# First chunk's two first half-width blocks written ahead of the third batch's recurrence

## The chip, the cores and the metric

The kernel runs on one core of a Trainium2 chip. The metric is the device time of one execution in microseconds (us). Engines are named as in the profile: PE is TensorE's matmul, PEld its weight load, DVE VectorE, ACT ScalarE, POOL GpSimd, SP SyncE, which issues most of the DMAs here.

## What is computed

An mLSTM recurrence over 4 batches, 8 heads, 768 steps and a head size of 40, and behind it two gated feed-forward layers on its output, all in float32:

```python
C = f_stab * C + i_stab * outer(v, k)     # per batch and head, step by step
n = f_stab * n + i_stab * k
y = sigmoid(o_gate) * (C @ q) / max(abs(n @ q), 1)
x = y as 3072 tokens x 320
x = (sigmoid(x @ w_gate) * (x @ w_val)) @ w_out       # d_ff 1536
h = x @ w_in                                          # d_ff 2048
out = (h * clip(h + 3, 0, 6) / 6) @ w_out2
```

## The kernel before

**Chunks.** The 768 steps are cut into 6 chunks (`NC`) of 128 steps. Inside a chunk the recurrence is done as matrix products, batch by batch; between chunks a state per batch is carried. A chunk gives 512 tokens (`T`): 4 batches of 128, batches 0 and 1 in the first half of the columns, 2 and 3 in the second.

**A batch of the recurrence** has three pieces. `att0`: scores on TensorE (L361), decays as scans on VectorE (L387), values scaled by ScalarE (L350) or VectorE (L352), the scores weighted on VectorE (L402). `att1`: the outputs on TensorE (L454, L469), the denominators (L491 to L495) and the gated product (L352, L503) on VectorE, the state (L521 to L529). `att2`: transposes on TensorE (L535), and the split into a high and a low part, `XH` on ScalarE (L540) and `XL` on VectorE (L541). Matmuls take their operands in such two parts, three products each.

**The first feed-forward layer** goes over 12 blocks (`F1`) of 128 hidden columns for each chunk. `m1_h(c, f, ts)` makes a block's two products from the tokens `ts` (16 matmuls in `h_pair`, L553 to L560, into two banks of PSUM), the sigmoid (L579, ScalarE), the product with the second bank (L580, VectorE), and the split of the result by `split_g` (L566 ScalarE, L567 VectorE). `m1_out` adds a block's 8 matmuls (L595, L605) into three accumulator banks; it is written one block behind `m1_h`. For chunk 0 the first 4 blocks are done in half widths: blocks 0 to 3 of `steps` take the tokens of batches 0 and 1, blocks 4 to 7 those of batches 2 and 3; from step 8 on a block has all 512 columns.

**Weights** arrive as 64-bit words of float64 and are turned into float32 by `scaled` (L100, ScalarE) and `to_f32` (L117, L120, VectorE), then split by `hi_in` (L141, L143, ScalarE) and `lo_in` (L149, L153, VectorE), or by `hi_out1` (L163) and `lo_out1` (L169, L172) for the output weights. `jobs` lists these conversions; `work(n, limit)` writes the next n of them, each with its fetch (L90).

**Order.** A first part, in `tc.manual_schedule()`, is ordered by hand: batches 0 and 1 of chunk 0, the first two input tiles (`w0`, `w1_`) and the first output tile (`wo_`), and last the state of the two batches. Each engine keeps the written order of these instructions. The rest is written in a loop over `steps`; a planner orders it for each engine by its own estimate of when operands are ready, and also puts such instructions between those of the hand-ordered part. In that loop `quota[i]` says how many pieces of the recurrence are written ahead of step i (batches 2 and 3 of chunk 0 first, then the next chunks'), and `work` follows each step.

**Buffers.** PSUM has 3 banks for blocks (`ps_mm`), 3 accumulators (`ps_acc`) and 2 for the recurrence (`ps_att`); the hand-ordered part takes all 8 in turn, and keeps one of `ps_mm` and one of `ps_acc` until `state(0, b)` has read them.

Of the kernel before, what the change touches and what calls it, by code (L numbers as in the profile page):

```python
# [26 lines left out]
T = B * L  # L27
F1 = 1536 // P
# [4 lines left out]
def mlstm_then_two_gated_ffn(  # L33
# [71 lines left out]
    def to_f32(r, u=None):  # L105

        lower = r.bitcast(I32).rearrange("p (n two) -> p two n", two=2)[:, 0, :]
        u = scaled(r) if u is None else u
        bits = gpool.tile([P, 640], I32, tag="bits", name="bits")
        nc.vector.tensor_scalar(  # L117
            out=bits, in0=u.bitcast(I32), scalar1=3, scalar2=None, op0=ALU.logical_shift_left
        )
        nc.vector.scalar_tensor_tensor(  # L120
            out=bits, in0=lower, scalar=29, in1=bits,
            op0=ALU.logical_shift_right, op1=ALU.bitwise_or,
        )
        return bits.bitcast(F32)
# [21 lines left out]
    def lo_in(w, x):  # L146
        wf = w.bitcast(F32)
        xm = x[:, 0:512].rearrange("p (j n) -> p j n", j=2)
        nc.vector.tensor_tensor(  # L149
            out=w[:, :, 384:640], in0=xm, in1=wf[:, :, 0:256], op=ALU.subtract  # L150
        )
        for j, a, b in halves_in:
            nc.vector.tensor_tensor(  # L153
                out=w[b, j, 256:384], in0=x[a, 512:640], in1=wf[a, j, 256:384], op=ALU.subtract
            )
# [4 lines left out]
    def hi_out1(key, x):  # L160

        w = new_slot(key)
        nc.scalar.copy(out=w[:, :, 0:320], in_=x.rearrange("p (j n) -> p j n", j=2))  # L163
        return w

    def lo_out1(w, x):
        wf = w.bitcast(F32)
        r = x.rearrange("p (j n) -> p j n", j=2)
        nc.vector.tensor_tensor(  # L169
            out=w[:, :, 320:384], in0=r[:, :, 256:320], in1=wf[:, :, 256:320], op=ALU.subtract  # L170
        )
        nc.vector.tensor_tensor(  # L172
            out=w[:, :, 384:640], in0=r[:, :, 0:256], in1=wf[:, :, 0:256], op=ALU.subtract
        )
# [399 lines left out]
    def m1_h(c, f, ts):  # L574
        n = ts.stop - ts.start
        banks = [ps_mm()[:, :n], ps_mm()[:, :n]]
        h_pair(slots["in", f], (1, c), banks, ts)
        g = gpool.tile([P, T], F32, tag="g", name="g")[:, :n]
        gate = nc.scalar.activation(out=g, in_=banks[0], func=AF.Sigmoid).ins  # L579
        nc.vector.tensor_tensor(out=g, in0=g, in1=banks[1], op=ALU.mult)  # L580
        gs[c, f, ts.start] = split_g(g)
        return gate

    def m1_out(c, f, ts):
        if f == 0 and ts.start == 0:
            acc1[c] = [ps_acc() for _ in range(3)]
        a = [bank[:, ts] for bank in acc1[c]]
        w = slots["out", f // 2][:, f % 2, :]
        gh, gl = gs.pop((c, f, ts.start))

        st, en = f == 0 and ts.start == 0, f == F1 - 1
        for m in range(2):
            hi, lo = w[:, m * P : (m + 1) * P], w[:, 384 + m * P : 384 + (m + 1) * P]
            for lhsT, rhs in ((hi, gh), (hi, gl), (lo, gh)):
                nc.tensor.matmul(  # L595
                    out=a[m], lhsT=lhsT, rhs=rhs, start=st and lhsT is hi and rhs is gh,
                    stop=en and lhsT is lo, skip_group_check=True,
                )

        tail = [  # L600
            dict(out=a[2], lhsT=w[:, 256:384], rhs=gh, start=st, stop=en),
            dict(out=a[2][0:64], lhsT=w[:, 256:320], rhs=gl, start=False, stop=False),
        ]
        for kw in tail if f == 0 else reversed(tail):
            nc.tensor.matmul(**kw, skip_group_check=True)  # L605

    def m1_end(c):
        a = acc1.pop(c)
        x2 = xpool.tile([P, 3, T], F32, tag="x2", name="x2")
        for m in range(2):  # L610
            nc.scalar.copy(out=x2[:, m, :], in_=a[m])

        sw = gpool.tile([P, T], F32, tag="g", name="sw")
        nc.scalar.copy(out=sw[0:64], in_=a[2][64:128])
        nc.scalar.copy(out=sw[64:128], in_=a[2][0:64])
        nc.vector.tensor_tensor(out=x2[:, 2, :], in0=sw, in1=a[2], op=ALU.add)
        nc.sync.dma_start(out=x2_dram[c], in_=x2)
# [28 lines left out]
    def work(count, limit):  # L646

        for _ in range(count):
            if len(jobs) > n_jobs - limit:
                src, use, key = jobs.pop()  # L650
                r = fetched.pop(0) if fetched else fetch(src)
                use(key, to_f32(r) if src.dtype == I64 else r)
# [9 lines left out]
    with tc.manual_schedule():  # L662
        qk_load(0, 0)
        vko_load(0, 0)
        qk_load(0, 1)
        raws = [fetch(jobs[-1][0])]
        vko_load(0, 1)
        for _ in stabilise(0, L):
            pass
        nc.sync.dma_start(out=fz_dram[0], in_=fz[:, 0, :])  # L670
        raws += [fetch(jobs[-2][0]), fetch(jobs[-3][0])]
        for b in range(2, B):
            qk_load(0, b)
            vko_load(0, b)
            dec_load(0, b)
        later = stabilise(L, S)
        first, second = spread(0), spread(1)
        next(later)
        next(later)
        next(first)  # L680
        transpose_rows(i_c, iT, range(0, 1))
        decays(0, 0, 0)
        next(first)
        next(later)
        next(later)
        decays(0, 0, 1)
        scores(0, 0, any_ps)
        value_ones(0, 0)
        values(0, 0, False)
        u = scaled(raws[0])  # L690
        values_end(0, 0, False)
        next(later)
        next(later)
        for n in range(2):
            weigh(0, 0, n)
            next(second)
        x0 = to_f32(raws[0], u)
        scores(0, 1, any_ps)
        for n in range(2):
            decays(0, 1, n)  # L700
        value_ones(0, 1)
        values(0, 1, False)
        values_end(0, 1, False)
        for b in range(2):
            out_gate(0, b)
        w0 = hi_in(jobs.pop()[2], x0)
        outputs(0, 0, any_ps)
        for n in range(2):
            weigh(0, 1, n)
        outputs(0, 1, any_ps)  # L710
        gated(0, 0, denominators(0, 0), False)
        u = scaled(raws[1])
        lo_in(w0, x0)
        gated(0, 1, denominators(0, 1), False)
        for b in range(2):
            opened = att2(0, b, any_ps)
        x1 = to_f32(raws[1], u)
        w1_ = hi_in(jobs.pop()[2], x1)
        u = scaled(raws[2])
        lo_in(w1_, x1)  # L720
        x2_ = to_f32(raws[2], u)
        wo_ = hi_out1(jobs.pop()[2], x2_)
        lo_out1(wo_, x2_)
        for b in range(2):
            state(0, b)

# [19 lines left out]
        pieces.append((c, B - 1, 2))  # L746
    n_first = len(tile_steps(0))

    quota = [2, 2] + [1] * 4 + [0, 1] * 4 + [1] * (n_first - 14) + [1, 1, 0, 1, 0, 1]
    quota += [1] * (len(steps) - len(quota))  # L750
    before = []
    for i, (c, f, ts) in enumerate(steps):
        if i == halves[0] - 1:
            for b in range(2):
                att_load(1, b)
                dec_load(1, b)
        for _ in range(quota[i]):
            if pieces:
                cp, b, piece = pieces.pop(0)
                if cp > 0 and b == 0 and piece == 0:  # L760
                    x_tiles((1, cp))
                with ExitStack() as queued:
                    for ins in opened if cp == 0 else ():
                        queued.enter_context(tc.issue_after(ins))
                    (att0, att1, att2)[piece](cp, b, ps_att)
                nxt = divmod(cp * B + b + 2, B)
                if cp > 0 and piece == 2 and nxt[0] < NC:
                    att_load(*nxt)
                    dec_load(*nxt)
        gate = m1_h(c, f, ts)  # L770
        if before:
            m1_out(*before)
            if before[1] == F1 - 1:
                m1_end(before[0])
        before = (c, f, ts)
        if c == 0:
            work(1 if i < 2 * halves[0] else 2, n_w1)
        elif c < NC - 1:

            with tc.issue_after(gate):  # L780
                work(c > 1 and f % 2 == 0, n_conv)
        elif f == 0:
            work(F2, n_conv)
        else:
            work(f > 1, n_jobs)
        if c == NC - 1 and f == 6:
            x_split(0)
# [125 lines left out]
```

## Time and profile before

| | us |
|---|---|
| runs shown | 871.9, 872.7, 873.03 (median 872.7) |
| profiled execution, its own time | 872.27 |
| its span in the profile | 870.5 |

The span is what the trace covers, from the first to the last event on the core; the execution's own time has 1.8 us around it. Times of rows are counted from the start of the span.

### The profile page before, as it was taken

How to read it: one execution, taken by the hardware profiler on the slowest of the kernel's cores; microseconds unless marked ns; L12 is line 12 of the kernel's file. 1: busy time of each engine (PE TensorE's matmuls, PEld its weight loads, DVE VectorE, ACT ScalarE, POOL GpSimd, SP SyncE). 2: the span in 40 equal slices, each digit the busy share in tenths (PEclk: the TensorE clock that was granted, in tenths of full speed). 3: DMA queues.
4: the chain of work that ended last, by engine and by line, in shares of the span. 5: the costliest groups of instructions: out<-in, count | busy, mean ns of one | idle time of the engine just before them, and what ended most of it. 6: DMA issues, size and time to landing. Idle time of an engine off the chain costs nothing.

```text
span 870.5 us, 16999 instructions
## 1 busy us (share of the span) xinstructions
PE 845.0 (97%) x7205; PEld 727.3 (84%) x7205; DVE 502.7 (58%) x898; ACT 358.6 (41%) x721; POOL 2.5 (0%) x8
## 2 busy tenths in 40 slices
PE   6599999999999999999999999999999999999998
PEld 6488778887878778878888888999999999999997
DVE  7899966665676666567545544344343353443433
ACT  3688634222333333332226445343343343433333
POOL 1000000000000000000000000000000000000000
PEclk9999999999999999999999999999999999999999
DMA  9636623331444355445103321001010010000000
GB/s 348 236 124 222 218 96 110 104 112 72 154 163 163 132 189 165 170 175 169 68 1 97 91 82 73 1 31 37 1 67 1 1 67 1 31 1 2 31 1 30
DMA packets 24923, 83.43 MB, mean 96 GB/s; under 512 B 2576, under 2 KB 5840, under 8 KB 24848
## 3 DMA queue, kind: packets, MB, share of 16 engines
q1 hardware_dynamic: 24800, 82.26, 27.7%
q8 instruction: 56, 0.92, 0.4%
q14 instruction: 19, 0.16, 0.1%
q10 hardware_dynamic: 48, 0.10, 0.0%
HBM read 68.35 MB, written 13.99 MB: 95 GB/s over the span
## 4 chain that ended last, share of the span: by engine, by line
PE 82%; DVE 10%; DMA 3%; issue 2%; ACT 2%; DVEq 0%; ACTq 0%; SPq 0%
PE mm L557 11%; PE mm L559 11%; PE mm L558 11%; PE acc L595 9%; PE mm L553 6%; PE mm L560 5%; PE acc L819 5%; PE acc L818 5%; PE acc L817 5%; PE acc L605 3%; DMA dec<-fz_dram 2%; PE att L361 2%; DVE dec L387 2%; PE att L819 2%; PE att L817 2%
## 5 line engine op out<-in xcount | busy, mean ns | idle before, releaser
L557 PE MATMUL mm<-xh,w 128*128 128x512 f32 (+1 forms) x520 | 195.7, 376 | 0.1
L558 PE MATMUL mm<-xl,w 128*128 128x512 f32 (+1 forms) x520 | 194.9, 375 | 0.0
L559 PE MATMUL mm<-xh,w 128*128 128x512 f32 (+1 forms) x520 | 194.8, 375 | 0.0
L566 ACT CAST gh<-g 128x512 fp32r<-128x512 f32 (+1 forms) x178 | 106.2, 597 | 214.1 <-DVE g L580 122.6
L567 DVE TENSOR_TENSOR gl<-g,gh 128x512 fp32r<-128x512 f32 (+1 forms) x178 | 117.6, 661 | 113.3 <-ACT gh L566 113.0
L799 DVE SCALAR_TENSOR_TENSOR g<-g,mm 128x512 f32<-128x512 f32 x96 | 66.0, 687 | 112.2 <-ACT g L798 112.2
L558 PEld LDWEIGHTS mm<-xl,w 128*128 128x128 f32 x520 | 98.5, 189 | 18.4
L559 PEld LDWEIGHTS mm<-xh,w 128*128 128x128 f32 x520 | 98.3, 189 | 18.5
L798 ACT ACTIVATE g<-mm,half 128x512 f32<-128x512 f32 x96 | 66.2, 690 | 112.1 <-PE mm L560 112.0
L557 PEld LDWEIGHTS mm<-xh,w 128*128 128x128 f32 x520 | 98.6, 190 | 14.4 <-issue 0.3
L595 PE MATMUL acc<-gh,w 128*128 128x512 f32 (+1 forms) x328 | 104.4, 364 | 2.2 <-ACT gh L566 2.2
L553 PE MATMUL mm<-xl,w 128*128 128x512 f32 (+1 forms) x260 | 104.2, 401 | 0.0
L560 PE MATMUL mm<-xh,w 128*128 128x512 f32 (+1 forms) x260 | 97.2, 374 | 0.0
L819 PE MATMUL acc<-w,gl 128*128 128x320 f32 x288 | 89.0, 309 | 0.0
L818 PE MATMUL acc<-w,gh 128*128 128x320 f32 x288 | 88.9, 309 | 0.0
L817 PE MATMUL acc<-w,gh 128*128 128x320 f32 x288 | 88.8, 308 | 0.0
L580 DVE TENSOR_TENSOR g<-g,mm 128x512 f32<-128x512 f32 (+1 forms) x82 | 50.5, 615 | 56.5 <-PE mm L560 55.9
L579 ACT ACTIVATE g<-mm 128x512 f32<-128x512 f32 (+1 forms) x82 | 44.7, 545 | 69.8 <-PE mm L560 69.4
L595 PEld LDWEIGHTS acc<-gh,w 128*128 128x128 f32 x328 | 60.4, 188 | 12.3 <-ACT gh L566 2.6
L595 PE MATMUL acc<-gl,w 128*128 128x512 f32 (+1 forms) x164 | 60.4, 369 | 1.6 <-DVE gl L567 1.4
L387 DVE TENSOR_TENSOR_SCAN dec<-dec,ident 128x512 f32<-128x512 f32 x40 | 47.7, 1214 | 23.5 <-DMA dec<-fz_dram 23.5
L553 PEld LDWEIGHTS mm<-xl,w 128*128 128x128 f32 x260 | 49.2, 189 | 9.1 <-issue 0.2
(155 smaller groups left out, 1078.2 us busy)
## 6 DMA issues: line engine op xcount, KB each, us to landing
raw<-in_w SPq DMA_DIRECT2D x20, 640.0 KB, 4.2
qk<-in_qkT SPq DMA_DIRECT2D x22, 512.0 KB, 5.1
vko<-in_vko SPq DMA_DIRECT2D x22, 480.0 KB, 4.9
dec<-fz_dram SPq DMA_DIRECT2D x20, 512.0 KB, 6.1
raw<-in_wo SPq DMA_DIRECT2D x14, 640.0 KB, 4.0
w_dram<-bits SPq DMA_DIRECT2D x16, 320.0 KB, 2.4
raw<-w_dram SPq DMA_DIRECT2D x16, 320.0 KB, 3.0
x_dram<-x SPq DMA_DIRECT2D x6, 768.0 KB, 4.5
```

The source lines that it names most:

```text
L553: nc.tensor.matmul(out=banks[j], lhsT=tail, rhs=xl[:, 2, :], start=True, stop=False)
L557: nc.tensor.matmul(out=banks[j], lhsT=hi, rhs=xh[:, k, :], start=False, stop=False)
L558: nc.tensor.matmul(out=banks[j], lhsT=hi, rhs=xl[:, k, :], start=False, stop=False)
L559: nc.tensor.matmul(out=banks[j], lhsT=lo, rhs=xh[:, k, :], start=False, stop=False)
L560: nc.tensor.matmul(out=banks[j], lhsT=tail, rhs=xh[:, 2, :], start=False, stop=True)
L566: nc.scalar.copy(out=gh, in_=g)
L567: nc.vector.tensor_tensor(out=gl, in0=g, in1=gh.bitcast(F32), op=ALU.subtract)
L595: nc.tensor.matmul(out=a[m], lhsT=lhsT, rhs=rhs, start=st and lhsT is hi and rhs is gh, stop=en and lhsT is lo, skip_group_check=True,)
L798: nc.scalar.activation(out=g[j], in_=banks[j], func=AF.Relu, scale=1.0 / 6.0, bias=half)
L817: nc.tensor.matmul(out=a, lhsT=gh[:, ts], rhs=hi, start=st, stop=False)
L818: nc.tensor.matmul(out=a, lhsT=gh[:, ts], rhs=lo, start=False, stop=False)
L819: nc.tensor.matmul(out=a, lhsT=gl[:, ts], rhs=hi, start=False, stop=en)
```

## The change

The half-width blocks 0 and 1 (`m1_h`) and the output product of block 0 (`m1_out`) are written inside the hand-ordered part: block 0 behind the low part of the second input tile, block 1 behind the high part of the first output tile, the output product behind that tile's low part. The loop over `steps` begins at step 2, with `before` set to step 1. The two conversions that `work` wrote behind steps 0 and 1 are written together ahead of the loop, and the six pieces of the recurrence that were written ahead of steps 0 to 3 (2, 2, 1, 1) are written ahead of steps 2 and 3 (3, 3).

```diff
--- before.py
+++ after.py
@@ -718,9 +718,13 @@
         w1_ = hi_in(jobs.pop()[2], x1)
         u = scaled(raws[2])
         lo_in(w1_, x1)
+
+        m1_h(0, 0, slice(0, T // 2))
         x2_ = to_f32(raws[2], u)
         wo_ = hi_out1(jobs.pop()[2], x2_)
+        m1_h(0, 1, slice(0, T // 2))
         lo_out1(wo_, x2_)
+        m1_out(0, 0, slice(0, T // 2))
         for b in range(2):
             state(0, b)
 
@@ -746,10 +750,11 @@
         pieces.append((c, B - 1, 2))
     n_first = len(tile_steps(0))
 
-    quota = [2, 2] + [1] * 4 + [0, 1] * 4 + [1] * (n_first - 14) + [1, 1, 0, 1, 0, 1]
+    quota = [0, 0, 3, 3] + [1] * 2 + [0, 1] * 4 + [1] * (n_first - 14) + [1, 1, 0, 1, 0, 1]
     quota += [1] * (len(steps) - len(quota))
-    before = []
-    for i, (c, f, ts) in enumerate(steps):
+    before = steps[1]
+    work(2, n_w1)
+    for i, (c, f, ts) in list(enumerate(steps))[2:]:
         if i == halves[0] - 1:
             for b in range(2):
                 att_load(1, b)
@@ -768,10 +773,9 @@
                     att_load(*nxt)
                     dec_load(*nxt)
         gate = m1_h(c, f, ts)
-        if before:
-            m1_out(*before)
-            if before[1] == F1 - 1:
-                m1_end(before[0])
+        m1_out(*before)
+        if before[1] == F1 - 1:
+            m1_end(before[0])
         before = (c, f, ts)
         if c == 0:
             work(1 if i < 2 * halves[0] else 2, n_w1)
```

## Rows read from the trace of the kernel before

**Rows 1.** The page, busy time, share of the span and instructions of each engine.

```profile
PE 845.0 (97%) x7205; PEld 727.3 (84%) x7205; DVE 502.7 (58%) x898; ACT 358.6 (41%) x721; POOL 2.5 (0%) x8
```

**Rows 2.** Windows: stretch, length, busy us (instructions) by engine, granted clock, DMA.

```profile
27.50:40.80 13.30, 5.93 (x119) 5.13 (x119) 13.21 (x27) 9.30 (x28) 0.00 (x0) 1.00 0.54 164
40.80:58.90 18.10, 17.76 (x230) 16.14 (x222) 17.27 (x40) 17.44 (x58) 0.00 (x0) 1.00 0.48 163
58.90:77.80 18.90, 16.74 (x242) 15.72 (x241) 18.25 (x42) 12.28 (x36) 0.00 (x0) 0.91 0.62 216
77.80:105.20 27.40, 27.26 (x247) 22.18 (x245) 26.50 (x55) 19.55 (x46) 0.00 (x0) 1.00 0.61 204
105.20:130.00 24.80, 24.80 (x258) 19.92 (x259) 16.55 (x33) 10.71 (x31) 0.00 (x0) 1.00 0.35 113
```

**Rows 3.** Timeline of PE from 25 us: start, length, what, idle before.

```profile
27.38 2.67 PE L361 MATMUL att<-early 40*128 40x128 f32 x16 [0.38 <-ACT iT L284]
35.65 0.36 PE L454 MATMUL att<-vi,early 128*32 128x41 f32 x8 [5.60 <-DVE early L402]
...
40.83 0.58 PE L553 MATMUL mm<-xl,w 128*128 128x256 f32 x1
...
41.42 0.41 PE L558 MATMUL mm<-xl,w 128*128 128x256 f32 x1
41.63 0.41 PE L559 MATMUL mm<-xh,w 128*128 128x256 f32 x1
...
43.28 0.28 PE L560 MATMUL mm<-xh,w 128*128 128x256 f32 x1
43.40 0.28 PE L553 MATMUL mm<-xl,w 128*128 128x256 f32 x1
...
58.97 0.39 PE L553 MATMUL mm<-xl,w 128*128 128x256 f32 x1
```

**Rows 4.** Groups of DVE instructions, 27.5 to 78 us: busy us, mean ns.

```profile
L120 DVE SCALAR_TENSOR_TENSOR bits<-raw,bits 128x640 int32<-128x640 int32 x10 | 8.1, 809 | 0.0
...
L117 DVE TENSOR_SCALAR bits<-u 128x640 int32<-128x640 int32 x10 | 4.8, 480 | 0.1
L149 DVE TENSOR_TENSOR w<-bits,w 128x512 fp32r<-128x512 f32 x6 | 4.0, 672 | 0.0
L153 DVE TENSOR_TENSOR w<-bits,w 64x128 fp32r<-64x128 f32 x12 | 3.4, 286 | 0.3
L580 DVE TENSOR_TENSOR g<-g,mm 128x256 f32<-128x256 f32 x8 | 3.3, 407 | 0.6 <-PE mm L560 0.6
L567 DVE TENSOR_TENSOR gl<-g,gh 128x256 fp32r<-128x256 f32 x7 | 2.9, 417 | 0.4 <-ACT gh L566 0.4
```

**Rows 5.** Timeline of DVE, third batch's second weighting and fourth batch's end.

```profile
38.38 0.67 DVE L402 TENSOR_TENSOR early<-att,early 128x512 f32<-128x512 f32 x1
...
57.27 0.56 DVE L541 TENSOR_TENSOR xl<-att,xh 128x384 fp32r<-128x384 f32 x1
```

**Rows 6.** Timeline of PE, 68 to 75 us.

```profile
68.42 0.28 PE L560 MATMUL mm<-xh,w 128*128 128x256 f32 x1
70.27 0.50 PE L595 MATMUL acc<-gh,w 128*128 128x256 f32 x2 [1.57 <-ACT gh L566]
71.36 0.39 PE L595 MATMUL acc<-gl,w 128*128 128x256 f32 x1 [0.58 <-DVE gl L567]
...
74.41 0.41 PE L558 MATMUL mm<-xl,w 128*128 128x256 f32 x1
74.62 0.41 PE L559 MATMUL mm<-xh,w 128*128 128x256 f32 x1
```

**Rows 7.** Timeline of ACT, 66 to 70 us.

```profile
66.27 0.68 ACT L529 COPY cst<-cst 40x164 f32<-40x164 f32 x2 [1.61 <-DVE cst L524]
66.97 0.39 ACT L579 ACTIVATE g<-mm 128x256 f32<-128x256 f32 x1
...
69.83 0.39 ACT L566 CAST gh<-g 128x256 fp32r<-128x256 f32 x1
```

## The prediction

> **What bounds the kernel now.** I read the page first: TensorE is busy 845.0 us of the span of 870.5 [rows 1]. So a gain can only come out of the places where TensorE is not packed. Next I cut the span into stretches by what runs in them (the windows view), and then read the timelines of the engines inside the stretches that are not packed.
>
> The stretches say this [rows 2]. From 77.8 us on TensorE is packed: 27.26 of 27.40 us, then 24.80 of 24.80. Behind that nothing touched by the change matters, as long as the blocks arrive no later. From 27.5 to 40.8 us TensorE is busy 5.93 of 13.30 and ScalarE 9.30, but VectorE is full: 13.21 of 13.30. From 40.8 to 58.9 all three are full: TensorE 17.76, VectorE 17.27, ScalarE 17.44 of 18.10. From 58.9 to 77.8 TensorE has holes again (16.74 of 18.90) and VectorE does not (18.25). And from 105.2 to 130 VectorE is down to 16.55 of 24.80: by then the weight conversions are done.
>
> The reader is to see that the end time is the moment at which TensorE's packed run begins, plus a constant. That moment depends on two gates. The first is the last instruction of the fourth batch's recurrence, L541 on VectorE, which ends at 57.27 + 0.56 = 57.83 [rows 5]. The second half of the tokens (blocks 4 to 7 of the list of steps) can't start without it, and block 4 does start at 58.97 [rows 3]. The second gate is the path from block 4 to about 77.8, with TensorE's waits of 1.57 and 0.58 us at 70.27 and 71.36 [rows 6].
>
> TensorE's idle stretch is plain in its timeline [rows 3]: scores of the third batch at 27.38, then nothing until 35.65, 5.60 us of it a wait for L402 on VectorE (the weighting of the third batch's scores). The first block starts at 40.83. Its matmuls follow each other by 0.21 us at first (41.42, 41.63) and by 0.12 later (43.28, 43.40): 256 columns at 1.2 and at 2.4 GHz.
>
> **The change part by part.**
>
> *Blocks 0 and 1 and the first output product.* They need the tokens of batches 0 and 1 and the first three weight tiles, which the hand-ordered section makes anyway. On TensorE they are 16 + 16 + 8 = 40 matmuls; at 0.12 us that is 4.8 us, which leaves the stretch from 40.8 on. It goes into 27.5 to 40.8, where 13.30 - 5.93 = 7.4 us are free. At 0.21 us each, as the first ones run now after the idle time, they take 8.4 us, 1.0 more than is free. I cost this at nothing because VectorE's queue covers it; if that cover were gone it would be 1.0 us.
>
> *What a block carries on ScalarE and VectorE.* On ScalarE one sigmoid and one cast, 0.39 us each [rows 7], so 2 x 0.78 = 1.56 us for two blocks. They go from a stretch in which ScalarE is full to one with 4.0 us free: hidden. On VectorE one product (0.407) and one subtraction (0.417) [rows 4], 2 x 0.82 = 1.65 us. They go from a full stretch into a full stretch. VectorE does no less work than before up to the fourth batch's L541, only in another order. Its idle time in both stretches is 0.09 + 0.83 = 0.92 us [rows 2], and that is all that a new order of the same work can win on VectorE itself. The lower bound is nothing. I take 0.5 us, the middle.
>
> *What is queued behind them.* In the hand-ordered section each engine keeps the written order. So the conversion of the third weight tile and the reading of the state (both written behind block 0 or 1) now wait for the block's chain: matmuls, sigmoid, product, cast, subtraction. Without overlap this adds 0.407 + 0.39 + 0.417 = 1.2 us a block, 2.4 us for two; with the third batch's scans filling the waits, only VectorE's own 1.65. The third batch's second L402, which now ends at 38.38 + 0.67 = 39.05 [rows 5], moves back by 1.7 to 2.4 us. The output product also has to wait until the state of batch 1 has been read out of its accumulator bank (three banks, one of them still held); that wait is new for a product written this early, but it lies in TensorE's idle time.
>
> *The two weight tiles written ahead.* `work(2)` now stands ahead of the third batch's three pieces. A tile costs VectorE 0.480 + 0.809 + 0.672 + 2 x 0.286 = 2.53 us [rows 4], two cost 5.1. If the planner takes them first, L402 moves back by up to 5.1 us more; if it uses them as filler, as it does today, by nothing. They are finished before the fourth batch's L541 in either order, so again the sum on VectorE is the same.
>
> *The fetches.* The queue of loads keeps its order: third and fourth weight tile, then the second output tile, then chunk 1's loads. The second output tile's fetch waits for the raw buffer of the tile whose conversion moved back by 1 to 2 us. I cost that at nothing: that tile's columns are wanted far later, at the third block's output product.
>
> *From the third batch's weighting to the fourth batch's L541* it is now 57.83 - 39.05 = 18.8 us. Blocks 0 and 1 lie between its links today; without them it has 1.65 us less on VectorE, 1.56 less on ScalarE, 4.8 less on TensorE. It starts 1.7 to 2.4 us later and is at least 1.65 shorter: 0 to 0.8 us of loss if only VectorE's share comes out, a gain if ScalarE's or TensorE's share was in series with it. I take the two as cancelling.
>
> The sum: 0 (TensorE, ScalarE) - 0.5 (VectorE's idle time) + 0 (start against length) = -0.5 us. The profiled execution took 872.27 us (span 870.5 and 1.8 around it), so 871.8; the median of the runs shown is 0.4 above that execution, so **872.2 us**. A measurement of this kernel tells about 0.2%, 1.7 us, from no change, so this counts as the same.
>
> A rule speaks against the change. TensorE is taken out of the full stretch and will have holes there, and after holes its matmuls run slowly: after the waits at 70.27 and 71.36 they follow by 0.21 us (74.41, 74.62), with a granted clock of 0.91 over that stretch [rows 2, 6]. The Trainium skill (TensorE: Matmul & The Clock Gate, What's actually happening) has it that the throttled state is the default and activity is what lifts it; the trace agrees with its 0.21 after idle time and 0.12 in packed stretches. What it would cost is the third rival below.
>
> **The rivals.**
>
> *Faster: the recurrence was held up by the blocks.* In 40.8 to 58.9 ScalarE and TensorE are as full as VectorE. If the recurrence of the two batches was slowed by queueing behind blocks 0 and 1 there, fourth-batch L541 and block 4 come earlier by 1.65 us (VectorE's share) up to 4.8 (TensorE's). A new order can also dissolve the hold-up at 68.42 to 71.36, worth 1.57 + 0.58 us of waits and about ten matmuls at 0.21 instead of 0.12 (0.9): 3.0 us. VectorE could then put off conversions, since it has 8.2 us free after 105.2. For it: three full engines. Against it: VectorE is full from 27.5 on, and it starts later. The gain is 2 to 4.8 us, 867.9 to 870.7, in the middle 869.3.
>
> *Slower: the third batch falls behind.* The blocks' chain and two tiles of weights ahead of it put L402 back by 1.7 to 2.4 + 5.1 = 7.5 us, and the fourth batch follows the third. Half of it is given back as the same work no longer lies in between. ScalarE's and VectorE's queues work in order, as the sigmoid at 66.97 shows: it stood behind L529, which had waited 1.61 us [rows 7]. It decides once L541 of the fourth batch ends more than 1.7 us after 57.83. Price 2 to 4 us: 874.7 to 876.7.
>
> *Slower: the clock.* Block 4 and the scores ahead of it start at half the clock after holes. Block 4's 16 matmuls cost 16 x 0.09 = 1.4 us more, and the scores (16 matmuls) as much at most: 1.4 to 2.8 us, 874.1 to 875.5.
>
> *The change does nothing:* the planner could leave all as it was around the recurrence, and blocks 0 and 1 just wait earlier. Time 872.7.
>
> **How the numbers follow.** Cancelling, as summed: 0.37. Nothing at all: 0.03. Faster: 0.36. Third batch behind: 0.17. Clock: 0.07. So faster by over 0.2% has 0.36, within 0.2% 0.40, slower 0.24. The range goes from 868.3 (the faster rival's outer end, less its last tenth) to 876.0 (most of the slower one). The likeliest case alone is 870.9 to 874.4.
>
> **What the profile after would show.** Right: blocks' matmuls at about 28 to 38 us, TensorE over 10 us busy in 27.5 to 40.8; VectorE full on both sides; the fourth batch's L541 within a microsecond and a half of 57.8, block 4 right behind it, and the first full-width block within that of 77.8. The faster rival: that L541 at 55 or earlier, or no wait at 70. The slower ones: L541 past 59.5, or 0.21 between block 4's matmuls. What would make me wrong most easily is the planner: it gives the rest of the work another order, and the stretch from 59 to 78 us hangs on which instruction stands ahead of which.

## The result, and the profile after

The changed kernel takes 881.82 us (median of 4 runs, 880.27 to 884.91) against 872.3 of the kernel before (4 runs): a ratio of 1.0116, 95% interval 1.0097 to 1.0134. I had forecast 872.2 and a range up to 876.0. It is slower, and by more than any rival said. The profiled execution is one of 880.27 us with a span of 878.5, so 8.0 us above the span before.

The stretches of the changed kernel (windows; columns as in [rows 2]):

```profile
27.50:40.80 13.30, 10.58 (x80) 9.38 (x83) 13.01 (x28) 9.62 (x30) 0.00 (x0) 0.98 0.47 165
40.80:58.90 18.10, 15.30 (x173) 12.00 (x165) 13.52 (x29) 12.43 (x40) 0.00 (x0) 0.69 0.56 183
58.90:77.80 18.90, 17.87 (x289) 16.02 (x289) 16.14 (x38) 11.30 (x33) 0.00 (x0) 0.86 0.32 110
77.80:105.20 27.40, 26.50 (x267) 22.02 (x266) 26.74 (x54) 21.37 (x54) 0.00 (x0) 1.00 0.61 197
105.20:130.00 24.80, 23.87 (x185) 18.61 (x187) 16.74 (x35) 11.99 (x34) 0.00 (x0) 1.00 0.34 122
```

Against [rows 2]: from 27.5 to 40.8 us TensorE now has 10.58 us of work instead of 5.93, as the change says. But from 40.8 to 58.9 VectorE is down from 17.27 to 13.52 and ScalarE from 17.44 to 12.43, and the granted clock is 0.69 instead of 1.00. All three engines had been full there; now all three wait for each other. VectorE's timeline in that time (start, length, what, idle before):

```profile
43.46 0.69 DVE L149 TENSOR_TENSOR w<-bits,w 128x512 fp32r<-128x512 f32 x1 [0.64 <-ACT w L141]
44.19 0.60 DVE L153 TENSOR_TENSOR w<-bits,w 64x128 fp32r<-64x128 f32 x2
44.82 0.82 DVE L120 SCALAR_TENSOR_TENSOR bits<-raw,bits 128x640 int32<-128x640 int32 x1
45.56 0.68 DVE L402 TENSOR_TENSOR early<-att,early 128x512 f32<-128x512 f32 x1
...
53.51 0.56 DVE L541 TENSOR_TENSOR xl<-att,xh 128x384 fp32r<-128x384 f32 x1 [0.34 <-ACT xh L540]
...
60.77 0.69 DVE L402 TENSOR_TENSOR early<-att,early 128x512 f32<-128x512 f32 x1 [4.70 <-PE att L361]
...
68.50 0.55 DVE L541 TENSOR_TENSOR xl<-att,xh 128x384 fp32r<-128x384 f32 x1
```

The third batch's second L402 ends at 46.24 instead of 39.05 [rows 5], 7.2 us later: between its first L402 (42.15) and this one VectorE now works on two further weight tiles (L149, L153, L120). The third batch's L541 follows at 53.51. Then VectorE stands idle for 4.70 us ahead of the fourth batch's second L402, for scores from TensorE, and the fourth batch's L541 ends at 69.05 instead of 57.83: 11.2 us later. TensorE in that time:

```profile
29.14 0.58 PE L553 MATMUL mm<-xl,w 128*128 128x256 f32 x1
...
37.97 0.39 PE L595 MATMUL acc<-gh,w 128*128 128x256 f32 x1 [1.59 <-ACT w L163]
...
44.62 0.36 PE L553 MATMUL mm<-xl,w 128*128 128x256 f32 x1 [0.22 <-DVE w L153]
...
50.20 0.39 PE L595 MATMUL acc<-gh,w 128*128 128x256 f32 x1 [2.58 <-ACT w L163]
...
50.57 0.41 PE L595 MATMUL acc<-gh,w 128*128 128x256 f32 x1
50.78 0.41 PE L595 MATMUL acc<-gl,w 128*128 128x256 f32 x1
...
57.00 0.35 PE L469 MATMUL mm<-vd,early 128*32 128x41 f32 x4
57.28 0.58 PE L559 MATMUL mm<-xh,w 128*128 128x256 f32 x1
57.79 0.35 PE L469 MATMUL mm<-vd,early 128*32 128x41 f32 x4
...
58.58 2.07 PE L361 MATMUL att<-early 40*128 40x128 f32 x8
...
70.19 0.38 PE L553 MATMUL mm<-xl,w 128*128 128x256 f32 x1
```

Block 0 starts 11.7 us earlier than in [rows 3] (29.14), block 1 9.2 us (34.20 instead of 43.40). Block 2 starts at 44.62, and its output product waits 2.58 us at 50.20 for L163, the conversion of the second output tile on ScalarE:

```profile
49.44 0.71 ACT L163 CAST w<-bits 128x640 fp32r<-128x640 f32 x1
```

Behind that wait matmuls follow by 0.21 us (50.57, 50.78). The fourth batch's second eight scores (58.58) stand behind block 3 and L469, the third batch's state, which alternate: four L469 and one of the block's matmuls take 0.79 us together (57.00, 57.79). The scores themselves need 2.07 us. Block 4 starts at 70.19 instead of 58.97, and the first full-width block (block 8) at 85.92 instead of 77.82: of 11.2 us, 3.1 are won back; the hold-up of [rows 6] is shorter this time (a wait of 0.87 us at 80.25 instead of 1.57 and 0.58, and no matmuls at 0.21 behind it). From block 8 to the end it takes as long as before: +8.1 at block 8, +8.0 at the end.

TensorE takes its matmuls in the order of its queue: the PSUM bank that these scores go to was free at 54.07, when the third batch's L541 had read it, and yet they started at 58.58. In the kernel before they start 0.13 us behind that L541:

```profile
47.65 0.53 DVE L541 TENSOR_TENSOR xl<-att,xh 128x384 fp32r<-128x384 f32 x1
```

```profile
48.31 1.16 PE L361 MATMUL att<-early 40*128 40x128 f32 x8
```

The Trainium skill says the same (TensorE: Matmul & The Clock Gate, the section on packing small matmuls: matmuls keep their order at start and end); the trace agrees with these 4.5 us.

### The profile page after: what moved, and what is told of

Read it like the earlier page. It is cut to its first block, busy times and chain, and to the rows that moved or that the text cites. A ratio compares the mean times of both kernels' runs of the same rounds, so it can differ in the third digit from the quotient of the medians.

```text
span 878.5 us, 16999 instructions
## 1 busy us (share of the span) xinstructions
PE 855.5 (97%) x7205; PEld 734.1 (84%) x7205; DVE 503.0 (57%) x898; ACT 358.9 (41%) x721; POOL 2.5 (0%) x8
## 4 chain that ended last, share of the span: by engine, by line
PE 83%; DVE 10%; DMA 3%; issue 2%; ACT 1%; DVEq 0%; SPq 0%
PE mm L557 11%; PE mm L558 11%; PE mm L559 11%; PE acc L595 9%; PE mm L553 6%; PE mm L560 5%; PE acc L823 5%; PE acc L822 5%; PE acc L821 5%; PE acc L605 3%; PE att L361 3%; DMA dec<-fz_dram 2%; DVE dec L387 2%; PE att L823 2%; PE att L821 2%
## 5 line engine op out<-in xcount | busy, mean ns | idle before, releaser
L559 PEld LDWEIGHTS mm<-xh,w 128*128 128x128 f32 x520 | 98.8, 190 | 18.8
L595 PE MATMUL acc<-gh,w 128*128 128x512 f32 (+1 forms) x328 | 106.2, 369 | 6.0 <-ACT w L163 4.2
```

The source lines that it names most:

```text
L559: nc.tensor.matmul(out=banks[j], lhsT=lo, rhs=xh[:, k, :], start=False, stop=False)
L595: nc.tensor.matmul(out=a[m], lhsT=lhsT, rhs=rhs, start=st and lhsT is hi and rhs is gh, stop=en and lhsT is lo, skip_group_check=True,)
```

## The experiments

Four theories: **Q**, the two conversions written ahead of the third batch put its weighting back; **M**, the blocks' chains in the hand-ordered part do; **P**, the fourth batch's scores stand in TensorE's queue behind block 3's matmuls, while VectorE is idle; **C**, the waits that a new order makes in TensorE bring its clock down, and that eats time. In one table, from each profile: the end of the third batch's second L402, the end of the fourth batch's L541, the start of block 8, the span; and the ratio to the kernel before, of all timed runs.

| kernel | L402 | L541 | block 8 | span | ratio (95%) |
|---|---|---|---|---|---|
| before | 39.05 | 57.83 | 77.82 | 870.5 | 1 |
| changed | 46.24 | 69.05 | 85.92 | 878.5 | 1.0116 (1.0097 to 1.0134) |
| blocks_only | 42.09 | 60.10 | 80.29 | 873.6 | 1.0025 (1.0000 to 1.0050) |
| blocks_only, second profile | 42.35 | 60.37 | 76.55 | 870.3 | one run, 872.13 us |
| order_only | 43.98 | 62.81 | 82.01 | 875.6 | 1.0062 (1.0039 to 1.0085) |
| two_tiles_ahead | 42.68 | 63.20 | 80.60 | 878.1 | 1.0089 (1.0065 to 1.0113) |
| tiles_behind_third | 42.03 | 62.56 | 81.20 | 878.4 | 1.0072 (1.0056 to 1.0088) |
| fourth_scores_first | 45.99 | 65.71 | 85.11 | 878.7 | 1.0086 (1.0064 to 1.0108) |
| block2_thrice | 46.45 | 63.92 | 82.30 | 875.6 | 1.0098 (1.0080 to 1.0116) |
| blocks_only_filled | 44.03 | 67.58 | 84.87 | 877.1 | 1.0076 (1.0057 to 1.0096) |
| blocks_only_filled3 | 42.06 | 66.70 | 83.97 | 877.9 | 1.0035 (1.0010 to 1.0060) |
| block0_only | 41.11 | 58.64 | 76.40 | 868.4 | 0.9987 (0.9978 to 0.9995) |
| block0_late | 39.70 | 60.01 | 82.80 | 873.0 | 1.0036 (1.0022 to 1.0049) |
| blocks_late | 39.61 | 65.42 | 83.64 | 876.7 | 1.0071 (1.0058 to 1.0083) |

**blocks_only.** The blocks stay moved, the rest is written in the old order.

```diff
-    before = steps[1]
-    work(2, n_w1)
+    before = steps[1]
+    ahead(2); work(1, n_w1); ahead(2); work(1, n_w1)   # ahead(n): the next n pieces
-    quota = [0, 0, 3, 3] + ...
+    quota = [0, 0, 1, 1] + ...
```

> The blocks stay in the hand-ordered part, but the pieces of the third and fourth batch and the two weight conversions are written in the old order again (two pieces, a conversion, two pieces, a conversion, one piece, block 2). Theory Q (the conversions written ahead of the third batch put its weighting back): the third batch's second L402 ends at 40 to 42 us (39.05 before, 46.2 after), the fourth batch's L541 by 60, total 869 to 874 us. Theory M (the two blocks' chains in the hand-ordered part hold VectorE and ScalarE up): L402 ends at 44 or later, total 878 to 882.

Measured: L402 at 42.09, L541 at 60.10, 873.79 us. As theory Q says, but for 0.1 us at both places. Moving the blocks costs the third batch 3.0 us at L402 and 0 to 0.5% in the total (2.4 us by the medians); the reordering of the rest, the only other difference to the changed kernel, costs 7.1 us (9.5 over the kernel before against 2.4, each by the medians of its own session).

**order_only.** The new order, with blocks 0 and 1 written behind the hand-ordered part.

```diff
-        m1_h(0, 0, slice(0, T // 2))
...
-        m1_out(0, 0, slice(0, T // 2))
+    m1_h(*steps[0]); m1_h(*steps[1]); m1_out(*steps[0])
     before = steps[1]
     work(2, n_w1)
```

> The change's order of everything else, but blocks 0 and 1 and the first output product are taken out of the hand-ordered part and written directly behind it. Theory Q: the third batch's second L402 again ends at 44 us or later, total 877 to 882 us. Theory M: L402 ends by 41, total 871 to 875.

Measured 877.34 us, L402 at 43.98, 0.02 us short of the bound given. The order alone makes 6.0 us of loss (against 871.35), over half.

**two_tiles_ahead.** Before, with the two conversions alone moved.

```diff
     before = []
+    work(2, n_w1)
     for i, (c, f, ts) in enumerate(steps):
...
-            work(1 if i < 2 * halves[0] else 2, n_w1)
+            work((i > 1) if i < 2 * halves[0] else 2, n_w1)
```

> The kernel before, with one thing done: the conversions of the third and fourth weight tile are written ahead of the loop, so ahead of the third batch's pieces, and steps 0 and 1 write none. Theory Q: the third batch's second L402 ends at 42 to 45 us, total 875 to 880 us. Theory M: no change, 871 to 874.

Measured 880.04 us, just past the upper edge of what Q gave, and L402 at 42.68. But not all of it comes the way Q meant. Up to block 8 only 2.8 us are lost; block 13 starts at 115.55 instead of 108.08, 7.5 later. TensorE there:

```profile
109.04 0.50 PE L595 MATMUL acc<-gh,w 128*128 128x512 f32 x1 [0.86 <-ACT gh L566]
111.16 0.50 PE L595 MATMUL acc<-gl,w 128*128 128x512 f32 x1 [1.62 <-DVE gl L567]
...
115.55 0.79 PE L553 MATMUL mm<-xl,w 128*128 128x512 f32 x1
116.14 0.63 PE L557 MATMUL mm<-xh,w 128*128 128x512 f32 x1
116.57 0.63 PE L558 MATMUL mm<-xl,w 128*128 128x512 f32 x1
```

Its product waits 0.86 and 1.62 us, and behind that 512 columns take 0.43 us (116.14, 116.57) where they take 0.23 in the packed stretch. Another order, another hole, and behind it matmuls at half the pace: the granted clock is 0.86 from 105.2 to 130, and 1.00 ahead of it.

**tiles_behind_third.** The changed kernel with `ahead(3)` ahead of `work(2, n_w1)` and a quota of [0, 0, 0, 3].

> The changed kernel with the two conversions written behind the third batch's three pieces instead of ahead of them; blocks 0 and 1 stay in the hand-ordered part. Theory Q: the second L402 ends at 41 to 43 us (46.2 in the changed kernel), the fourth batch's L541 by 62, total 870 to 877 (the lower end where the clock stays up). If the cost is in writing three pieces together or in the blocks: L541 past 65, total 878 to 882.

Measured 879.17 us: a miss for Q in the total. L402 (42.03) is where Q put it, L541 (62.56) 0.6 past its bound, block 8 3.4 us behind before; then the same hole as above, block 13 at 116.42 instead of 108.08. So the place of the two tiles decides when the third batch is weighted, and does not by itself decide the end.

**fourth_scores_first.** `quota = [0, 0, 4, 2] + ...` in the changed kernel.

> The changed kernel with the fourth batch's first piece (its scores) written ahead of block 2 instead of ahead of block 3. Theory P (the scores' second bank stands on TensorE behind block 3's matmuls, at 1.2 GHz, while VectorE is idle 4.7 us): the scores come right behind the third batch's L541, the fourth batch's L541 comes at 63 to 66 us instead of 69, total 876 to 879. If only the conversions ahead of the third batch matter (Q alone): 880 to 883.

Measured 879.46 us, between the ranges of the two theories. L541 comes 3.3 us earlier, as P said; block 8 only 0.8. TensorE's timeline:

```profile
62.99 0.49 PE L535 MATMUL att<-ident,yo 128*128 128x128 f32 x2 [4.22 <-DVE yo L503]
...
67.77 0.58 PE L553 MATMUL mm<-xl,w 128*128 128x256 f32 x1
68.14 0.41 PE L557 MATMUL mm<-xh,w 128*128 128x256 f32 x1
68.36 0.41 PE L558 MATMUL mm<-xl,w 128*128 128x256 f32 x1
...
73.98 0.39 PE L553 MATMUL mm<-xl,w 128*128 128x256 f32 x1
```

TensorE had waited 4.22 us ahead of the fourth batch's transposes, and block 4 ran at 0.21 us a matmul. It starts 2.4 us earlier than in the changed kernel (67.77), block 5 no earlier (73.98 against 73.92), with the granted clock at 0.73 from 58.9 to 77.8 instead of 0.86. The time was given back to the clock.

**block2_thrice, blocks_only_filled, blocks_only_filled3.** `h_pair` of one block (two in the second) is called again with the same operands, so as to keep TensorE at work where it waits.

```diff
-        h_pair(slots["in", f], (1, c), banks, ts)
+        for _ in range({(0, 2, 0): 3}.get((c, f, ts.start), 1)):
+            h_pair(slots["in", f], (1, c), banks, ts)
```

(`{(0, 1, 0): 2, (0, 3, 0): 2}` and `{(0, 3, 0): 2}` in the two others.)

> The changed kernel with block 2's 16 matmuls made three times (same sums), so that TensorE works through the 2.58 us in which it now waits for L163 at 50.20 us. Theory C: the matmuls up to the fourth batch's L541 run at 0.12 instead of 0.21, it ends 2 to 4 us earlier than 69.05, total 876 to 880. If only queues matter: not earlier, total 881 to 885.

> blocks_only with the 16 matmuls of block 1 and those of block 3 made twice (the second time into the same banks from the start, so the sums are the same): 32 matmuls more on TensorE, put where blocks_only has it waiting ahead of its two stretches at 0.21 us a matmul (37.6 to 47.6 and 60.6 to 70.5 us). Theory C (the clock after TensorE's waits is what eats the gain): both stretches run at 0.12, the fourth batch's L541 ends 1 to 2 us earlier than 60.1, block 8 starts at 76 to 78.5 instead of 80.3, total 868 to 872, so not above the kernel before in spite of more work. If the clock matters little: 32 more matmuls make it 874 to 878.

> The same with block 3 alone made twice. Theory C: the stretch at 60.6 to 70.5 us runs at 0.12, the one at 37.6 stays; block 8 starts at 77.5 to 79.5, total 870 to 873. If the clock matters little: 874 to 877.

Measured 880.02, 878.25 and 873.23 us. The first is just past the upper edge of theory C: 32 matmuls more and not slower than the changed kernel, L541 5.1 us earlier. The second is a miss: L541 comes at 67.58 instead of 60.10, and the matmuls of blocks 2 and 3 run at 0.21 us from 49.7 to 61.7. The third says neither: six of its ten runs lie at 871.1 to 873.6 us and four at 877.7 to 879.7, and in its profile, one of the upper group, the granted clock is 0.50 from 40.8 to 58.9, in spite of the matmuls added there. In all three the planner gave what follows another order, so that they can't tell the clock from the order; I don't count them.

**block0_only.** blocks_only with block 0 alone in the hand-ordered part; block 1 and the product are written behind it, among the third batch's pieces.

```diff
         m1_h(0, 0, slice(0, T // 2))
         x2_ = to_f32(raws[2], u)
         wo_ = hi_out1(jobs.pop()[2], x2_)
-        m1_h(0, 1, slice(0, T // 2))
         lo_out1(wo_, x2_)
-        m1_out(0, 0, slice(0, T // 2))
...
     ahead(2); work(1, n_w1); ahead(2)
+    m1_h(*steps[1]); m1_out(*steps[0])
     work(1, n_w1)
```

> blocks_only with block 0 alone in the hand-ordered part; block 1 and the first output product stand where they stood before. Only one block's chain lies ahead of the third batch: the second L402 ends at 39.5 to 41 us by theory M's share (39.05 with none, 42.1 with two), total 869 to 874. If the hand-ordered blocks cost nothing by themselves: the same as blocks_only, 872 to 875.

Measured 870.02 us over 11 runs against 871.41 over 21: 0.9987, 0.9978 to 0.9995. It beats both kernels, by little; L402, at 41.11, is 0.1 us past what was expected. Its lines, VectorE's timeline and the windows:

```profile
40.44 0.67 DVE L402 TENSOR_TENSOR early<-att,early 128x512 f32<-128x512 f32 x1
...
58.08 0.56 DVE L541 TENSOR_TENSOR xl<-att,xh 128x384 fp32r<-128x384 f32 x1
```

```profile
27.50:40.80 13.30, 9.80 (x52) 8.60 (x52) 13.01 (x27) 9.15 (x28) 0.00 (x0) 0.86 0.50 163
40.80:58.90 18.10, 18.10 (x283) 15.71 (x283) 16.76 (x40) 16.56 (x54) 0.00 (x0) 0.92 0.46 158
58.90:77.80 18.90, 18.45 (x255) 16.91 (x256) 18.69 (x42) 13.00 (x39) 0.00 (x0) 1.00 0.60 219
```

The fourth batch's L541 ends at 58.64, 0.8 us behind [rows 5], and the stretch from 58.9 on has 18.45 us of work on TensorE at a clock of 1.00, against 16.74 at 0.91 [rows 2].

**block0_late, blocks_late.** The same two kernels with the block (the blocks and the product) written behind `lo_out1(wo_, x2_)`, so that no conversion stands behind a block.

> block0_only with block 0 written behind the conversion of the third weight tile (behind lo_out1), so that in the hand-ordered part nothing but the state stands behind it. Theory M's share (the block's chain puts the tile's conversion and with it L402 back): the second L402 ends at 39 to 40.5 us (41.1 in block0_only), total 868 to 870.5. If block0_only's gain hangs on that place: 870 to 873.

> blocks_only with both blocks and the product written behind lo_out1. Theory M: the second L402 ends at 39 to 41 us instead of 42.1, total 868 to 872. If the blocks' own cost lies in the clock of TensorE and not in the order of VectorE: runs at two levels again, 870 to 878.

Measured 875.02 and 878.49 us, outside every range given. L402 comes at 39.70 and 39.61, nearly as early as before, as M said it would, and both are slower than the kernels with L402 at 41.11 and 42.09: M has the place of L402 right, and that place does not decide the time. In blocks_late the fourth batch's L541 comes 25.8 us after L402, in the kernel before 18.8, and VectorE waits for the fourth batch's second eight scores as in the changed kernel:

```profile
56.38 0.69 DVE L402 TENSOR_TENSOR early<-att,early 128x512 f32<-128x512 f32 x1 [3.60 <-PE att L361]
```

The granted clock is 0.71 there from 40.8 to 58.9; in block0_late it is 0.81 from 58.9 to 77.8.

**blocks_only_again.** The same program as blocks_only, for a second profile.

> blocks_only unchanged, for a second profile. Its ten runs lie at two levels, 870.1 to 872.2 us with a mean clock of 0.996 to 0.998 and 875.4 to 878.0 with 0.984 to 0.990; the profile shown is of the upper level. Theory C: if this execution is of the lower level, the same instructions in the same order have no stretch at 0.21 us from 60.6 to 70.5, the fourth batch's L541 ends at 57 to 60 us and block 8 starts 3 to 5 us before 80.3. If the two levels come from elsewhere (a DMA, a later stage), the stretches up to block 8 are alike.

Of the ten timed runs of blocks_only five lie at 870.1 to 872.2 us and five at 875.4 to 878.0 (medians 871.3 and 876.8; the kernel before 871.35). The first profile is of the upper group (873.6 us of span, its own time 875.39), the second of the lower (870.3, 872.13). TensorE's timeline in the first, ahead of block 4 and in it:

```profile
57.91 0.41 PE L535 MATMUL att<-ident,yo 128*128 128x128 f32 x2 [0.72 <-DVE yo L503]
```

```profile
60.56 0.41 PE L595 MATMUL acc<-gl,w 128*128 128x256 f32 x1
...
61.42 0.41 PE L595 MATMUL acc<-gh,w 128*128 128x256 f32 x1
...
63.98 0.58 PE L553 MATMUL mm<-xl,w 128*128 128x256 f32 x1
64.36 0.41 PE L557 MATMUL mm<-xh,w 128*128 128x256 f32 x1
64.57 0.41 PE L558 MATMUL mm<-xl,w 128*128 128x256 f32 x1
```

and in the second:

```profile
58.17 0.41 PE L535 MATMUL att<-ident,yo 128*128 128x128 f32 x2 [0.72 <-DVE yo L503]
```

```profile
60.27 0.28 PE L595 MATMUL acc<-gl,w 128*128 128x256 f32 x1
...
60.75 0.28 PE L595 MATMUL acc<-gh,w 128*128 128x256 f32 x1
...
62.16 0.39 PE L553 MATMUL mm<-xl,w 128*128 128x256 f32 x1
...
62.74 0.28 PE L557 MATMUL mm<-xh,w 128*128 128x256 f32 x1
62.86 0.28 PE L558 MATMUL mm<-xl,w 128*128 128x256 f32 x1
```

Up to 58 us the two are the same to 0.3 us, and so is the wait of 0.72. Behind it, scores and transposes only; then the first execution goes on at 0.21 to 0.22 us a matmul, the second at 0.12. Block 4 starts at 63.98 and 62.16, block 5 at 70.28 and 66.02, block 8 at 80.29 and 76.55. VectorE and ScalarE do the same in the same order. Theory C holds here without another order to confuse it: one such stretch costs 3.7 us at block 8 and 3.3 at the end. The fourth batch's L541 (60.10 and 60.37) does not move with it, against what I expected, since it lies ahead of the stretch.

## Why the prediction was wrong

**What held.** The blocks went where I put them: TensorE's free time from 27.5 to 40.8 took them, at 0.21 us for block 0, and ScalarE's share was hidden there (9.62 of 13.30). The end time follows the start of block 8, plus a constant, in the changed kernel: +8.1 and +8.0. In eleven of the fourteen profiles the way from there to the end is 792.0 to 793.9 us; in block0_late it is 790.2, in two_tiles_ahead and tiles_behind_third 797.5 and 797.2. The fourth batch's L541 is the first gate: block 4 never starts ahead of it.

**The step that failed** is the cancelling of the third batch's later start against a shorter way from its L402 to the fourth batch's L541, which rested on VectorE doing the same work in another order and staying full. The start moved 7.2 us, not 1.7 to 2.4: blocks alone give 3.0 (blocks_only), the two tiles alone 3.6 (two_tiles_ahead), and I had taken the tiles for filler. My sum for a block's chain also left out the sigmoid (0.39 us), which it names; with it two blocks come to 3.2 us, close to the 3.0. And the way grew from 18.8 to 22.8 us instead of shrinking. VectorE did not stay full: it had 4.6 us idle from 40.8 to 58.9, 3.4 of them ahead of the fourth batch's two L402, because the scores stood in TensorE's queue.

**The second term** that was wrong is the clock. My sum put it at nothing; the rival had it at 1.4 to 2.8 us and a chance of 0.07. The new order has waits of 1.59 and 2.58 us in TensorE, and its 256-column matmuls followed each other by 0.21 us between 50.6 and 62.5. The trace agrees with the rule of the Trainium skill that I had set beside it (TensorE: Matmul & The Clock Gate, What's actually happening), that the throttled state is the default and activity lifts it. Measured on one program, one such stretch is 3.3 us of span (5.5 between the medians of the two groups).

**The rivals.** "The third batch falls behind" named the mechanism, its point of decision (L541 past 59.5) and its sign; at 2 to 4 us it was half the size. What it missed is that a late third batch and a lower clock came together (0.69 from 40.8 to 58.9): late data left holes in TensorE, matmuls behind them ran at 0.21 us, and the next data came later still. That each fed the other is my reading of the rows; no run shows it apart from the order.

**What stays open.** How the 9.5 us of the changed kernel divide between order and clock: nothing tried here holds the order and keeps the clock up in it. The orders tried give 868 to 879 us of span. All that they lose is lost ahead of block 13: from its start to the end all fourteen profiles take 760.3 to 762.8 us. But no single place ahead of it explains them: two_tiles_ahead and tiles_behind_third lose more than half of it between block 8 and block 13, the changed kernel nearly all ahead of block 8. The clock goes with the loss without being shown as its cause: from 45 to 120 us it is 1.00 in block0_only and in the second profile of blocks_only, which end no later than the kernel before (0.98 there), and 0.89 to 0.95 in the others but block2_thrice, which has 0.98 and 32 matmuls more. Why the same wait of 0.72 us is followed by a lower clock in one execution and not in another isn't settled either.

## What to carry to other kernels

Idle time on one engine is not by itself room for work as long as the next engine that the work passes through is full: ask what each instruction behind it in that queue feeds. When work is taken out of a packed stretch of TensorE, count the holes that it leaves, and allow for half the clock behind each: here it came in one execution of a program and not in another. Move one piece at a time: block 0 alone was worth a gain of 0.13%, the whole edit a loss of 1.16%.

## What was not expected of the hardware

One program ran at two levels 5.5 us apart (0.6%), with the clock of TensorE as the only difference seen in two profiles. The mean clock of an execution sorts most of these runs (0.996 and above against 0.984 to 0.990), but not the last one, which had 0.990 and 870.3 us: it counts where the clock is low, and in a stretch in which TensorE sets the pace each 0.12 us become 0.21.
